# When batch 2's k is loaded, and when k's second piece is turned, in sliding-window attention with a gated feed-forward on one core

## The chip, the cores and the metric

The kernel runs on one core of one Trainium2 chip. The metric is the time of one execution on the device, in microseconds (us), and the figure that counts is the median of the runs. The core has engines that work side by side, each through its own queue in order: TensorE (PE, matrix products, with its weight loads PEld), VectorE (DVE), ScalarE (ACT), GpSimd (POOL) and SyncE (SP). In this kernel SP computes nothing. It issues transfers, and a transfer that waits on SP holds up every transfer behind it.

## The reference

Inputs q, k and v are [8 batches, 8 heads, 576 positions, 64] in float32.

```python
scores = scale * np.matmul(q, k.transpose(0, 1, 3, 2))      # scale = 1/8
mask = (rel >= 0) & (rel < 64)                               # rel = query position - key position
scores = np.where(mask, scores, -1000000000.0)
attn = exp(scores - max) / sum                               # softmax over the keys
o = np.matmul(attn, v)
x = o.transpose(0, 2, 1, 3).reshape(4608, 512)
h = x @ w_in                                                 # w_in 512 x 2048
out = (h * np.cos(h)) @ w_out                                # w_out 2048 x 512
```

A query sees only itself and the 63 positions before it. In blocks of 64 positions, a query block needs its own key block and the one before.

## The kernel before

**Two halves, interleaved.** The feed-forward runs over nine stages (`mt` 0 to 8) of 512 rows of x. A stage first makes h (line 443, `h_ps`) with the cosine gate (lines 589 and 592), and then the output product (line 604, `out_ps`). The attention of batch b is worked out inside an earlier stage: batch 1 inside the output product of stage 0, batch 2 inside that of stage 1, and so on. Its pieces are slipped between the matmuls by a list of planned times. `at(time, fn, ...)` puts a step on the list, and `pump(time)` calls whatever is due. A planned time is a place in the order only. It decides after which instruction a step stands on its engine, and nothing is held until that time on the chip.

**Groups.** The unit of attention is a pair of heads p and a query block j. Units are handled in groups of three or four. One group goes through these steps:

- scores on PE (line 305, `s_ps`), reading qT and kT, or qX and kX from batch 2 on
- masking and the row minimum on DVE (line 329, `s` and `negm`)
- the exponential with its sum on ACT (line 340, `e` and `den`)
- the reciprocal on DVE (line 347, `rden`)
- the normalisation `g_norm` on POOL (line 354, w = e * rden). The first three groups of batch 1 and the tail of batch 0 have it on DVE
- the transposition of w. Groups in the list `DIRECT` go through PE (line 363, `tw_ps`) and a copy on DVE. The others go through a transposing transfer from SP (line 366, `wT<-w`)
- the values product on PE (line 381, `o_ps`), copied as xT for the feed-forward stage

Groups are counted from `n_first`, so "group 9" of the change is the tenth counted from the tail of batch 0. It is a group of three units of batch 1, and it is the seventh group that POOL normalises after it has issued batch 2's q.

**Loading q and k.** From batch 2 on, `load_chunk` (line 159; issue at line 165) loads q and k of a batch in five chunks of 128 positions each. It is issued from POOL's queue. An issue takes POOL about 0.9 us, and the norms of line 354 stand in the same queue. `load_v` (line 168, issue at line 171) loads v the same way, after batch 1's norms. Part of v is then shifted by half a block (`v<-v`): for batch 1 by two transfers from SP (line 180), which the values product of stage 1 waits for.

**Turning.** `turn` (line 246, issue at line 250) transposes what was loaded, from SP: all of q as `qX` in one transfer of 20 blocks, then k as `kX` in two. The first piece holds chunks 0 and 1 (8 blocks), the second chunks 2 to 4 (12 blocks). The scores of a batch come in two lots. The first lot reads the first piece of kX alone, and the second lot, some 6 us later, reads the second piece as well. Before the change the first piece of k is planned just behind q, and the second for `t0 + 2.5`, a few steps later. In between stand the transposing transfers of the previous batch's last groups (two for batch 2, four in the later stages), and behind them the stores of the finished output (line 463).

**Where batch 2's k stood.** Batch 2's q chunks were planned from 4.0 in steps of 0.5, k's chunks 0 to 3 right behind them, and chunk 4 at 26.9. On POOL this gives: five q loads, four k loads, six norms of batch 1, the fifth k load, one norm (group 9), two norms, then v.

Of the kernel before, what the change touches and what calls it, by code (L numbers as in the profile page):

```python
# [40 lines left out]
T = 2 * Q  # L41
# [23 lines left out]
def kernel(  # L65
# [401 lines left out]
    def at(time, fn, *args):  # L467
        plan.append((time, len(plan), fn, args))
# [10 lines left out]
    for t in range(B - 1):  # L479
        last = max(i for i, units in enumerate(groups) if units[0][0] == t + 1)  # L480
        time = T * t + Q - 1.4
        for i in range(last + 1 - n):
            time += PACE * len(groups[n - 1]) if i else 0
            if t and i == 4:
                time = max(time, T * t + Q + 4.3)
# [16 lines left out]
    for b in range(1, B):  # L502
        t0 = T * (b - 1)
        if b > 1:
            for i, name in enumerate(("q", "k")):
                for c in range(NC):
                    time = 4 + 0.5 * (c + NC * i) if b == 2 else t0 - T + 8 + 0.9 * (c + NC * i)
                    if i and c > (3 if b == 2 else 1):
                        time = 26.9 if b == 2 else t0 - T + 22.5 + 1.5 * (c - 2)
                    at(time, load_chunk, name, b, c)  # L510
                for c, (lo, hi) in enumerate(((0, 2), (2, NC)) if i else ((0, NC),)):
                    at(t0 + 2.5 if c else t0 - (5.8 if b > 2 else 3.4) + 0.1 * i, turn, name, b, lo, hi)
            for c in range(5):
                at(t0 + 3.5 + 0.9 * c, load_v, b, c)
            for time, part in ((13.5, 0), (19.9, 2), (21.7, 3)):
                at(t0 + time, spread_v, b, part, None)
# [5 lines left out]
    for mt in range(1, n_mt):  # L522
        for p in range(PAIRS):
            time = max(ready[b, p - p % 2 + i // TU, j] for i in range(2 * TU) for b, j in (divmod(mt * TU + i % TU, NU),))
            time = max(time, 25.5) if mt == 1 else T * mt - (8.01 if mt == n_mt - 1 else 1.01)
# [118 lines left out]
```

## Time and profile before

| what | before |
|---|---|
| median of three runs | 306.38 us (304.9, 306.38, 306.77) |
| the profiled execution's own time | 305.0 us |
| its span, first to last instruction | 302.9 us |
| PE busy | 286.5 us, 95% of the span |
| ACT busy | 235.0 us, 78% |
| DVE busy | 221.4 us, 73% |
| POOL busy | 172.2 us, 57% |
| granted TensorE clock | 1.000 |
| software queue (loads from POOL) | 18.06 MB, 79.3% of 16 engines' span |
| hardware queue (transfers from SP) | 24.98 MB, 47.3% |

The profile is of one execution. Its own time stands 1.4 us under the median of the three runs, so a difference that is worked out inside the trace is applied to both. The span leaves out 2.1 us around the program. A timeline row has the start in us, the duration in us, the engine, the line, the operation and what is written and read, how many instructions are merged in the row, and in brackets the engine's idle time before it and what ended that. "x3" with one duration is the stretch that three instructions took together. An engine with a "q" (SPq) is the queue that issues: its duration is the issue, and the transfer lands later. The row "DMA to landing" gives the least, the median and the longest time from issue to landing of the transfers asked for.

### The profile page before, as it was taken

To read this page: it belongs to the slowest core of one execution; us is meant where nothing else is said; L and a number is where in the kernel's file an instruction comes from. 1 tells how busy PE (TensorE), PEld (TensorE's weight loads), DVE (VectorE), ACT (ScalarE), POOL (GpSimd) and SP (SyncE) were. 2 spreads that over 40 slices of the span, in tenths; PEclk is the share of its full clock that TensorE was granted. 3 is DMA by queue.
4 is the path that set the end of the run, shared out by engine and by line. 5 is a ranking of instruction groups with operands and counts; after the bars stand their busy time and mean duration, and the time that the engine had idled before them with its cause. 6 is when DMAs were issued, how large, how long until landed. Compare 5 with 4: busy or idle time off the path is not lost.

```text
span 302.9 us, 8058 instructions
## 1 busy us (share of the span) xinstructions
PE 286.5 (95%) x2726; PEld 148.4 (49%) x2762; DVE 221.4 (73%) x852; ACT 235.0 (78%) x783; POOL 172.2 (57%) x204
## 2 busy tenths in 40 slices
PE   3789997999999999999999999989999999999996
PEld 2568743544454445444544454444544454454443
DVE  3899897778967897789678967896789778236701
ACT  5897898678997799879987998799869996116600
POOL 8997369792799368945995599549803620000000
PEclk9999999999999999999999999999999999999999
DMA  8999999999999999999999999999993470012011
GB/s 171 172 197 210 207 163 164 115 145 142 220 164 144 177 181 173 131 184 195 93 159 151 232 154 162 141 220 161 171 198 119 89 176 16 3 69 72 0 69 69
DMA packets 164841, 43.75 MB, mean 144 GB/s; under 512 B 153920, under 2 KB 160064, under 8 KB 164800
## 3 DMA queue, kind: packets, MB, share of 16 engines
q0 software_dynamic: 99360, 18.06, 79.3%
q1 hardware_dynamic: 65296, 24.98, 47.3%
q8 instruction: 21, 0.34, 0.5%
q14 instruction: 20, 0.16, 0.2%
q10 hardware_dynamic: 144, 0.20, 0.2%
HBM read 36.70 MB, written 9.44 MB: 152 GB/s over the span
## 4 chain that ended last, share of the span: by engine, by line
PE 67%; DMA 15%; POOL 6%; DVE 6%; issue 4%; ACT 0%; SPq 0%; POOLq 0%; DVEq 0%
PE h_ps L443 31%; PE out_ps L604 28%; DMA v<-in_v_dram 5%; DMA kX<-k 4%; POOL w L354 4%; DMA k<-in_k_dram 3%; DMA v<-v 3%; PE o_ps L381 2%; DVE s L329 2%; PE s_ps L305 2%; PE out_ps L455 1%; POOL v L171 1%; DMA q<-in_q_dram 1%; DVE negm L325 1%; PE tw_ps L363 1%
## 5 line engine op out<-in xcount | busy, mean ns | idle before, releaser
L604 PE MATMUL out_ps<-w_out,gT 128*128 128x512 bf16 x542 | 124.0, 379 | 1.7 <-issue 1.3
L443 PE MATMUL h_ps<-xT,w_in 128*128 128x512 bf16 x497 | 111.0, 379 | 1.1 <-issue 0.2
L354 POOL TENSOR_TENSOR w<-e,rden 128x512 bf16<-128x512 f32 (+1 forms) x75 | 73.0, 984 | 59.9 <-DVE rden L347 56.3
L592 DVE TENSOR_TENSOR gT<-h_ps,sin 128x512 bf16<-128x512 f32 x128 | 84.9, 688 | 30.2 <-ACT sin L589 30.2
L340 ACT ACTIVATE e<-s,negm 128x128 f32<-128x128 f32 x256 | 99.2, 403 | 1.9 <-DVE negm L329 1.8
L589 ACT ACTIVATE sin<-h_ps 128x512 f32<-128x512 f32 x128 | 73.7, 599 | 28.6 <-PE h_ps L443 28.1
L604 PEld LDWEIGHTS <-gT 128*128 128x128 bf16 x560 | 52.7, 98 | 60.5 <-issue 0.4
L443 PEld LDWEIGHTS <-w_in 128*128 128x128 bf16 x512 | 49.9, 98 | 59.1
L329 DVE CUSTOM_DVE_ANT_0 s<-s_ps,mask 128x128 f32<-128x128 f32 x256 | 57.9, 283 | 1.9 <-PE s_ps L305 1.7
L340 ACT ACTIVATION_READ_ACCUMULATOR e<-s,negm 128x1 f32 x256 | 51.9, 203 | 0.0
L171 POOL DMA_DIRECT2D v<-in_v_dram x40 | 34.1, 870 | 6.6 <-DMA w_out<-in_moe_w_out_dram 4.2
L117 ACT COPY out_sb<-out_ps 128x512 f32<-128x512 f32 (+1 forms) x18 | 10.5, 582 | 24.9 <-PE out_ps L604 19.3
L165 POOL DMA_DIRECT2D k<-in_k_dram x30 | 26.4, 893 | 1.7 <-DMA v<-in_v_dram 1.6
L165 POOL DMA_DIRECT2D q<-in_q_dram x30 | 25.4, 886 | 3.1 <-DMA w_out<-in_moe_w_out_dram 3.1
L117 DVE CAST xT<-o_ps 128x512 bf16<-128x512 f32 x28 | 18.3, 679 | 9.6 <-PE o_ps L381 9.3
L117 DVE COPY out_sb<-out_ps 128x512 f32<-128x512 f32 x18 | 12.3, 681 | 14.9 <-PE out_ps L604 14.9
L329 DVE DVE_READ_ACCUMULATOR2_ANT negm<- 128x1 f32 x256 | 20.9, 82 | 0.0
L347 DVE RECIPROCAL rden<-den 128x4 f32<-128x4 f32 (+1 forms) x80 | 13.5, 171 | 9.6 <-ACT e L340 7.7
L420 PE MATMUL h_ps<-xT,w_in 128*128 128x256 bf16 x128 | 15.5, 273 | 0.0
L420 PEld LDWEIGHTS <-w_in 128*128 128x128 bf16 x128 | 12.0, 98 | 1.4
L117 DVE COPY v<-v 64x1024 bf16<-64x1024 bf16 (+1 forms) x19 | 11.4, 601 | 0.4
L426 ACT ACTIVATE sin<-h_ps 128x512 f32<-128x512 f32 x16 | 9.1, 597 | 2.9 <-PE h_ps L420 2.9
(60 smaller groups left out, 187.5 us busy)
## 6 DMA issues: line engine op xcount, KB each, us to landing
out_dram<-out_sb SPq DMA_DIRECT2D x16, 512.0 KB, 7.7
v<-in_v_dram POOLq DMA_DIRECT2D x32, 128.0 KB, 6.2
q<-in_q_dram POOLq DMA_DIRECT2D x24, 128.0 KB, 8.7
k<-in_k_dram POOLq DMA_DIRECT2D x24, 128.0 KB, 7.9
w_in<-in_moe_w_in_dram POOLq DMA_DIRECT2D x2, 768.0 KB, 11.1
w_out<-in_moe_w_out_dram POOLq DMA_DIRECT2D x1, 1024.0 KB, 12.9
w_out<-in_moe_w_out_dram POOLq DMA_DIRECT2D x2, 512.0 KB, 15.5
wT<-w SPq DMA_TRANSPOSE x58, 5.0
```

Source lines behind the costliest of these rows:

```text
L117: {"a": nc.scalar.copy, "p": nc.gpsimd.tensor_copy}.get(engine, nc.vector.tensor_copy)(out, in_)
L165: nc.gpsimd.dma_start(out=st[name, b][:n, c].rearrange("p (h d) -> p h d", h=H), in_=src.rearrange("h p d -> p h d"))
L171: nc.gpsimd.dma_start(out=vt.rearrange("p (h d) -> p h d", h=H), in_=v[b, :, c * 128:c * 128 + n, :].rearrange("h p d -> p h d"))
L329: nc.vector.tensor_tensor_reduce(out=s[:, u], in0=s_ps[:, u], in1=mask[:, 2 - j % 2 if j else 0], scale=-scale if b else -1.0, scalar=BIG, ...
L340: nc.scalar.activation(e[:, u], s[:, u], AF.Exp, bias=negm[:, u:u + 1], scale=1.0 if n < n_first else -1.0, accum_out=den[:, u:u + 1])
L347: nc.vector.reciprocal(out=rden[:, 0:len(groups[n])], in_=den[:, 0:len(groups[n])])
L354: (nc.gpsimd if engine == "p" else nc.vector).tensor_tensor(out=w[:, 0:u], in0=e[:, 0:u], op=ALU.mult, in1=rden[:, 0:u].unsqueeze(2).to_br ...
L420: nc.tensor.matmul(out=st["h0", i][:, e], lhsT=w_in_sb[:, ks, ff * 128:ff * 128 + 128], rhs=st["xT", 0][:, ks, half], start=ks + e == 0, s ...
L443: nc.tensor.matmul(out=st["h", ff], lhsT=w_in_sb[:, ks, ff * 128:ff * 128 + 128], rhs=st["xT", mt][:, ks], start=start, stop=stop)
L589: nc.scalar.activation(sin, h_ps, AF.Sin, bias=math.pi / 2.0)
L592: nc.vector.tensor_tensor(out=gt[:, e], in0=h_ps, in1=sin, op=ALU.mult)
L604: nc.tensor.matmul(out=o_ps[e], lhsT=gT[ff // 2][:, ff % 2, ms * 128:ms * 128 + 128], rhs=w_out_sb[:, ff], start=ff == 0, stop=ff == n_ff - 1)
```

## The change

Two conditions in the plan are altered. Batch 2's k chunks 0 to 3 no longer follow its q. All five are planned at 27.1 to 27.5. On POOL this puts all of them behind the seventh norm, that of group 9, and ahead of the last two norms of batch 1. And `turn` of k's second piece is planned 0.1 behind the first piece, in every stage, where it was planned for `t0 + 2.5`.

```diff
                     time = 4 + 0.5 * (c + NC * i) if b == 2 else t0 - T + 8 + 0.9 * (c + NC * i)
-                    if i and c > (3 if b == 2 else 1):
-                        time = 26.9 if b == 2 else t0 - T + 22.5 + 1.5 * (c - 2)
+                    if i and (b == 2 or c > 1):
+                        time = 27.1 + 0.1 * c if b == 2 else t0 - T + 22.5 + 1.5 * (c - 2)
                     at(time, load_chunk, name, b, c)
                 for c, (lo, hi) in enumerate(((0, 2), (2, NC)) if i else ((0, NC),)):
-                    at(t0 + 2.5 if c else t0 - (5.8 if b > 2 else 3.4) + 0.1 * i, turn, name, b, lo, hi)
+                    at(t0 - (5.8 if b > 2 else 3.4) + 0.1 * i + 0.1 * c, turn, name, b, lo, hi)
```

The order of the instructions on PE, DVE and ACT stays the same, instruction for instruction, and no instruction is added or taken away. The orders of POOL and SP become these:

```
POOL, batch 2     before: q x5, k x4, norm x6, k, norm, norm x2, v x5
                  after:  q x5, norm x7, k x5, norm x2, v x5
SP, batch 2       before: qX, kX first, wT x2, kX second, stores
                  after:  qX, kX first, kX second, wT x2, stores
SP, batches 3, 4, 6   before: qX, kX first, wT x4, kX second, stores
                      after:  qX, kX first, kX second, wT x4, stores
SP, batches 5, 7  before: qX, kX first, wT x4, kX second, stores
                  after:  qX, kX first, wT, kX second, wT x3, stores
```

## The prediction

> **What bounds the kernel now.** PE is busy 95% of the span, so I read PE's waits first: only what PE waits for can be won. The rows give the waiting work, the releaser, the total in us, the times and the longest.
>
> ```profile
> PE tw_ps L363 <- POOL w L354: 1.5, 3, 0.9
> ...
> PE s_ps L305 <- DMA kX<-k: 0.6, 1, 0.6
> ...
> PE o_ps L381 <- DMA v<-v: 0.4, 1, 0.4
> ```
>
> These three are the waits that the change can touch, 2.5 us together. Next, PE's timeline, for their places and for the times at which PE asks for what the change moves.
>
> ```profile
> 49.34 0.34 PE L363 MATMUL tw_ps<-ident,w 128*128 128x128 bf16 x3 [0.86 <-POOL w L354]
> 50.12 0.34 PE L363 MATMUL tw_ps<-ident,w 128*128 128x128 bf16 x3 [0.45 <-POOL w L354]
> ...
> 53.36 0.60 PE L381 MATMUL o_ps<-wT,v 128*64 128x64 bf16 x26 [0.44 <-DMA v<-v]
> ...
> 58.43 0.69 PE L381 MATMUL o_ps<-wT,v 128*64 128x64 bf16 x32
> ...
> 72.33 0.64 PE L305 MATMUL s_ps<-kX,qX 64*64 64x128 bf16 x32
> ...
> 78.19 0.75 PE L305 MATMUL s_ps<-kX,qX 64*64 64x128 bf16 x40
> ...
> 88.35 1.20 PE L381 MATMUL o_ps<-wT,v 128*64 128x64 bf16 x64
> ...
> 202.16 0.75 PE L305 MATMUL s_ps<-kX,qX 64*64 64x128 bf16 x40 [0.62 <-DMA kX<-k]
> ...
> 211.59 1.20 PE L381 MATMUL o_ps<-wT,v 128*64 128x64 bf16 x64
> ```
>
> PE stands 0.86 + 0.45 = 1.31 us for two norms of batch 1, 0.44 for the shifted v, and much later 0.62 for the second piece of kX. Now POOL, which does the norms and issues the loads.
>
> ```profile
> 44.86 3.54 POOL L165 DMA_DIRECT2D k<-in_k_dram  x4
> 48.46 2.39 POOL L354 TENSOR_TENSOR w<-e,rden 128x384 bf16<-128x384 f32 x3
> 51.09 0.83 POOL L354 TENSOR_TENSOR w<-e,rden 128x384 bf16<-128x384 f32 x1 [0.23 <-DVE rden L347]
> 52.18 1.61 POOL L354 TENSOR_TENSOR w<-e,rden 128x384 bf16<-128x384 f32 x2 [0.27 <-DVE rden L347]
> 53.73 0.74 POOL L165 DMA_DIRECT2D k<-in_k_dram  x1
> 54.67 0.83 POOL L354 TENSOR_TENSOR w<-e,rden 128x384 bf16<-128x384 f32 x1 [0.20 <-DVE rden L347]
> 57.04 2.04 POOL L354 TENSOR_TENSOR w<-e,rden 128x512 bf16<-128x512 f32 x2 [1.54 <-PE tw_ps L363]
> 59.02 4.26 POOL L171 DMA_DIRECT2D v<-in_v_dram  x5
> ```
>
> Three norms start with no wait right behind four k issues: they were ready and stood behind the issues.
>
> **Part 1, the norms ahead of k.** The reciprocal that the third norm needs is done at 47.97 + 0.17 = 48.14, those of the first two before it:
>
> ```profile
> 47.97 0.17 DVE L347 RECIPROCAL rden<-den 128x3 f32<-128x3 f32 x1
> ```
>
> With POOL free at 44.86 and 0.8 us a norm (2.39 / 3), the first two are done by 48.14, and the third by about 48.9. PE asks for the first at 49.34 - 0.86 = 48.48, and for the second at 49.67 less those 0.86. Both waits go: **-1.31 us**, if PE can use them. The next lock is the shifted v. In the chain of waits its transfer runs from 45.39 for 7.84 us, beside the four k loads; the landing row of these four follows.
>
> ```profile
> 45.39 7.84 DMA v<-v
> ...
> DMA to landing us min/median/max: 7.6/7.9/8.6
> ```
>
> It lands at 53.23, and PE would now ask at 53.36 - 0.44 - 1.31 = 51.61. If the landing stays, the whole 1.31 turns into a longer wait there, and the part is worth 0. If it comes by 51.61, the part is worth 1.31 + 0.44 = 1.75. Without the four k loads the engines have less to move from 44.86 on. If the k loads took half of the last 3.2 us (my estimate: two streams at the end of it), v lands near 51.6. That is the value I take.
>
> The next thing late is a `wT` that the last 32 value products at 58.43 need. Its norm is the sixth. Norms five and six need a reciprocal whose exponential is among the last of ACT's unbroken run:
>
> ```profile
> 50.42 0.40 ACT L340 ACTIVATE e<-s,negm 128x128 f32<-128x128 f32 x1
> ```
>
> That run ends near 50.9 and cannot start earlier, so the two norms end at about 51.2 + 1.61 = 52.8. SP issues the `wT` then, where it did so at 53.82:
>
> ```profile
> 53.82 2.55 SPq L366 DMA_TRANSPOSE wT<-w  x1
> 56.69 3.11 SPq L250 DMA_TRANSPOSE qX<-q  x1
> 59.95 1.26 SPq L250 DMA_TRANSPOSE kX<-k  x1
> 61.31 2.90 SPq L366 DMA_TRANSPOSE wT<-w  x2
> 64.39 5.77 SPq L250 DMA_TRANSPOSE kX<-k  x1
> ...
> 183.13 1.25 SPq L250 DMA_TRANSPOSE kX<-k  x1
> 184.48 5.92 SPq L366 DMA_TRANSPOSE wT<-w  x4
> 190.57 5.12 SPq L250 DMA_TRANSPOSE kX<-k  x1
> ```
>
> The landing row of the one at 53.82, and below it that of all `wT`:
>
> ```profile
> DMA to landing us min/median/max: 4.1/4.1/4.1
> ...
> DMA to landing us min/median/max: 2.3/5.0/9.2
> ```
>
> With 4.1 it lands at 56.9 to 57.0. PE, 1.75 earlier, asks at 56.68: 0.3 given back. Part 1 is worth **1.45 us** (0 to 1.75).
>
> **Part 2, k comes later.** The seventh norm needs a reciprocal behind the xT copy on DVE, which moves with PE. I put the norm at 52.9 to 53.7. The five k issues then run from 53.7 to about 58.0 (4 x 0.89 + 0.74). They cost PE nothing as long as kX is in time. The last two norms end at 60.0, and v is issued from 60.0, 1.0 later than before. v's cover: its landing row, and the DVE copy that reads chunks 1 to 3.
>
> ```profile
> DMA to landing us min/median/max: 6.2/7.1/9.0
> ...
> 72.81 0.67 DVE L117 COPY v<-v 64x1536 bf16<-64x1536 bf16 x1
> ```
>
> Chunk 3 issued at 62.7 lands at 69.8, or 71.7 with the longest; the copy stands at 72.81 - 1.45 = 71.4. So v costs 0, or 0.3 us at the worst of its own rows.
>
> For kX the rows of k: the lone fifth load of before, at 53.73, and all chunk loads; then the second piece at 64.39, and all turns.
>
> ```profile
> DMA to landing us min/median/max: 4.0/4.0/4.0
> ...
> DMA to landing us min/median/max: 3.4/8.3/15.4
> ...
> DMA to landing us min/median/max: 11.8/11.8/11.8
> ...
> DMA to landing us min/median/max: 3.8/6.9/11.8
> ```
>
> The first piece needs chunk 1, issued at 54.6: in at 58.6 (4.0) to 62.9 (8.3). With 6.9 its turn lands at 65.5 to 69.8, and PE asks at 72.33 - 1.45 = 70.88: in time. The second piece needs chunk 4, issued at 57.2: in at 61.2 to 65.5. SP, free of the two `wT` that stood ahead, issues it at about 62 to 66. Even with the 11.8 of before, it lands at 74 to 77.8, against 78.19 - 1.45 = 76.74. I take 4.0 to 6 for the k loads, since POOL issues no other load between 48 and 59, and a landing at 75: cost **0** (0 to 1.1 by the median load, 7.7 by the longest).
>
> [...]
>
> **Part 3, the second turn ahead of the `wT`.** At 183.13 the first piece is issued, and the second, 7.4 us later, lands so that PE stands 0.62 us. Issued at about 184.4 with the longest landing of 11.8 it is in by 196.2, four us ahead of 200.1 (202.16 - 0.62 - 1.45): **-0.62 us**. What it displaces: four `wT`, each later by the 5.12 of that issue at most. The last, issued before 190.4, then goes at 195.5 and lands with 9.2 at 204.7, and its values product stands at 211.59. For batch 2, two `wT` are issued by 72 and land by 81 against 88.35. The stores behind them stay where they were, since the same issues stand ahead of them. SP may wait for k's last chunk in front of the `wT`; the margins of 7 us cover that.
>
> **The sum.** -1.45 - 0.62 = -2.07 us. On the profiled execution that is 305.0 - 2.1 = 302.9 us. The median of the runs is 1.4 above that execution, so 306.38 - 2.1 = **304.3 us**, 0.7% less. The most that these edits can win is 1.31 + 0.44 + 0.62 = 2.37 us.
>
> **The rivals.**
> - *k too late (slower).* The place is the second lot of batch 2's scores. Any landing of the second piece after 76.74 is a stall; from 76.74 + 2.07 = 78.8 on the kernel is slower than before. With the longest k landing, chunk 4 is in at 57.2 + 15.4 = 72.6, the turn lands at 84.4, PE stalls 7.7 us, and the time is 306.38 - 2.1 + 7.7 = 312.0. For it: v and q loads follow k in the same queue, and the turn took 11.8 here. Against it: 15.4 is the largest of all chunk loads, and the lone load of this place took 4.0.
> - *The same, small.* A landing between 76.74 and 78.8 eats part of the gain: 304.3 to 306.4, about 305.4.
> - *The shifted v does not hurry.* If v lands at 53.23 anyway, part 1 is worth 0, and only the 0.62 stays: 305.8. For it: 7.84 us may be the transfer's own time beside q loads.
>
> **How the numbers follow.** Forecast 0.52, small lateness 0.18, v unhurried 0.18, k too late 0.12. The three runs spread by 1.9 us, and 1% (3.1 us) is about what a measurement of this kernel can tell from no change. The forecast's gain lies inside that, and only the runs' spread or a gain outside these edits carries it below 303.3: faster 0.17. Of k too late, and of losses that I have not seen, 0.13 goes over 309.4. The rest, 0.70, is within. The range takes in 2.37 with some spread (302.6), and above the forecast the small lateness, v unhurried and the near half of the slower rival (308.0).
>
> **What would show it.** Right: no wait of `tw_ps` on POOL near 48 to 50, `v<-v` in by about 51.7, the five k issues at 53.7 to 58, the second kX in before 76.7, no wait at the scores near 200, all later stages shifted by 1.4 to 1.8. Wrong: PE waiting for kX at either lot of batch 2's scores, or for v at 51.6, or for a `wT` at the last values, or a new wait on a displaced store or `wT`.

## The result and the profile after

The changed kernel takes 302.35 us (median of five executions) where the kernel before takes 306.38. The ratio is 0.9893, with a 95% interval of 0.9857 to 0.9929. The ratios here and below leave out executions more than 1.5% longer than the fastest of the same kernel (here the one of 307.52 us), which the medians keep. The profiled executions compare like this: 305.0 us before and 302.35 after, spans 302.9 and 300.6. Between these two traces the gain is therefore 2.3 us, against 2.07 forecast. The medians are 4.0 apart, and where the rest comes from is told below.

PE's waits in the changed kernel (waiting work, releaser, total us, times, longest):

```profile
PE o_ps L381 <- DMA v<-v: 0.3, 1, 0.3
...
PE tw_ps L363 <- POOL w L354: 0.2, 1, 0.2
```

Of the 2.5 us of three waits, 0.5 is left, and kX is in the list no more. PE's timeline at the places of the prediction:

```profile
48.49 0.50 PE L363 MATMUL tw_ps<-ident,w 128*128 128x128 bf16 x6
...
51.74 0.60 PE L381 MATMUL o_ps<-wT,v 128*64 128x64 bf16 x26 [0.29 <-DMA v<-v]
...
56.81 0.69 PE L381 MATMUL o_ps<-wT,v 128*64 128x64 bf16 x32
...
70.71 0.64 PE L305 MATMUL s_ps<-kX,qX 64*64 64x128 bf16 x32
...
76.57 0.75 PE L305 MATMUL s_ps<-kX,qX 64*64 64x128 bf16 x40
...
86.74 1.20 PE L381 MATMUL o_ps<-wT,v 128*64 128x64 bf16 x64
...
199.85 0.75 PE L305 MATMUL s_ps<-kX,qX 64*64 64x128 bf16 x40
```

The two transpositions that stood 0.86 and 0.45 us now run as one piece. The later rows stand 1.6 us earlier than before (58.43 to 56.81, 72.33 to 70.71), and near 200, where PE no longer waits, they come to stand 2.3 us earlier (202.16 to 199.85). POOL and SP in the same stretch:

```profile
46.84 2.54 POOL L354 TENSOR_TENSOR w<-e,rden 128x384 bf16<-128x384 f32 x3 [1.55 <-DVE negm L329]
49.71 0.83 POOL L354 TENSOR_TENSOR w<-e,rden 128x384 bf16<-128x384 f32 x1 [0.33 <-DVE rden L347]
51.77 2.40 POOL L354 TENSOR_TENSOR w<-e,rden 128x384 bf16<-128x384 f32 x3 [1.23 <-DVE negm L329]
54.11 4.26 POOL L165 DMA_DIRECT2D k<-in_k_dram  x5
```

```profile
45.07 1.29 SPq L180 DMA_DIRECT2D v<-v  x2
50.56 4.03 SPq L366 DMA_TRANSPOSE wT<-w  x2
54.90 4.16 SPq L250 DMA_TRANSPOSE qX<-q  x1
63.00 4.99 SPq L250 DMA_TRANSPOSE kX<-k  x2
68.09 3.36 SPq L366 DMA_TRANSPOSE wT<-w  x2
```

The norms now wait for their inputs, with POOL free ahead of them. On SP the gap between the end of qX's issue (59.06) and 63.00 is the wait for k's chunk 1. The landing rows, in this order: the shifted v, the five k loads, and the second turn of kX for batch 2:

```profile
DMA to landing us min/median/max: 5.9/5.9/5.9
...
DMA to landing us min/median/max: 3.9/7.8/8.3
...
DMA to landing us min/median/max: 8.6/8.6/8.6
```

The shifted v takes 5.9 us where it took 7.84. Issued second at about 45.75, it lands at 51.6. The second kX is issued at 65.4 and lands at 74.0, 2.6 us ahead of PE.

### The profile page after: what moved, and what is told of

It reads as the page before. It is cut to its first block, busy times and chain, and to the rows that moved or that the text cites. A ratio compares the mean times of both kernels' runs of the same rounds, so it can differ in the third digit from the quotient of the medians.

```text
span 300.6 us, 8056 instructions
## 1 busy us (share of the span) xinstructions
PE 286.6 (95%) x2726; PEld 148.8 (50%) x2762; DVE 221.4 (74%) x852; ACT 234.5 (78%) x783; POOL 172.1 (57%) x204
## 4 chain that ended last, share of the span: by engine, by line
PE 78%; DMA 10%; DVE 4%; POOL 3%; issue 3%; SPq 0%; ACT 0%; POOLq 0%; DVEq 0%
PE h_ps L443 36%; PE out_ps L604 34%; DMA v<-in_v_dram 5%; DMA k<-in_k_dram 3%; PE s_ps L305 3%; PE o_ps L381 2%; DMA v<-v 2%; POOL w L354 2%; PE out_ps L455 1%; DVE xT L117 1%; DVE s L329 1%; PE tw_ps L363 1%; PE tk_ps L214 0%; DVE qT L236 0%; DVE negm L325 0%
## 5 line engine op out<-in xcount | busy, mean ns | idle before, releaser
L340 ACT ACTIVATION_READ_ACCUMULATOR e<-s,negm 128x1 f32 x256 | 48.1, 188 | 0.0
L117 ACT COPY out_sb<-out_ps 128x512 f32<-128x512 f32 (+1 forms) x18 | 10.2, 565 | 24.9 <-PE out_ps L604 19.3
```

The costliest lines, as they stand in the source:

```text
L117: {"a": nc.scalar.copy, "p": nc.gpsimd.tensor_copy}.get(engine, nc.vector.tensor_copy)(out, in_)
L340: nc.scalar.activation(e[:, u], s[:, u], AF.Exp, bias=negm[:, u:u + 1], scale=1.0 if n < n_first else -1.0, accum_out=den[:, u:u + 1])
```

## The experiments

The theory was the prediction's: PE waited for norms that stood behind k's issues, then for a shifted v that shared the DMA engines with k, and later for a turn that stood behind four `wT`. The rivals were that one of the two edits alone carries the gain, that the shifted v takes its own time, and that late loads are made up.

In the table, "full clock" is the median of those executions whose mean granted TensorE clock was above 0.997, and "lower" counts those with 0.984 to 0.994. The ratios are against the kernel before, timed on the same chip in the same rounds.

| run | median us | ratio, interval | full clock | lower |
|---|---|---|---|---|
| before, in three rounds of runs | 305.83, 305.40, 304.98 | | 304.89, 304.88, 304.59 | 18 of 29, 9 of 29, 10 of 28 |
| changed kernel, repeated | 303.13 | 0.9911 (0.9884 to 0.9938) | 303.13 | 0 of 6 |
| k loads only | 304.51 | 0.9982 (0.9954 to 1.0010) | 304.03 | 4 of 12 |
| turn only | 304.61 | 0.9972 (0.9949 to 0.9995) | 304.43 | 5 of 12 |
| norms on DVE | 304.75 | 0.9979 (0.9952 to 1.0005) | 304.44 | 4 of 12 |
| k behind all norms | 305.90 | 0.9984 (0.9956 to 1.0012) | 304.54 | 8 of 12 |
| k behind v | 313.39 | 1.0252 (1.0221 to 1.0282) | none | 5 of 5 |
| q behind the fourth norm | 306.34 | 1.0015 (0.9982 to 1.0047) | 305.19 | 6 of 12 |
| filler on PE | 305.59 | 1.0008 (0.9984 to 1.0033) | 305.59 | 0 of 12 |
| q behind the third norm | 307.73 | 1.0065 (1.0031 to 1.0099) | 304.54 | 10 of 12 |
| changed kernel, repeated | 302.57 | 0.9913 (0.9885 to 0.9941) | 302.57 | 0 of 11 |
| k split | 303.15 | 0.9927 (0.9900 to 0.9954) | 303.15 | 0 of 12 |

**The changed kernel again.**

> The changed kernel once more, beside its parts. Both theories: ratio to before near 0.989, time 302.1 to 303.3 us, no wait of tw_ps on POOL near 48 to 50, v<-v in near 51.6, no wait for kX.

The time held. But the profiled execution, the longest of the six at 303.96 us, shows PE waiting 1.60 us for the shifted v, where the first one showed 0.29:

```profile
53.31 0.60 PE L381 MATMUL o_ps<-wT,v 128*64 128x64 bf16 x26 [1.60 <-DMA v<-v]
```

There v itself had come later, so that the shift was issued at 47.03 and 47.71, not 45.07 and 45.75, and it landed at 53.17 although it took only 5.5 us. PE's row stands at 53.31, where the kernel before had it at 53.36: in this execution v eats all that the norms had won. So the shifted v is the lock that is left. The three profiles of the changed kernel fit the view that its landing spreads the executions (302.35 us with a wait of 0.29, 303.96 with 1.60, 304.18 with 1.64), but three traces do not show it for the others.

**One part alone: the loads.**

```diff
-                    if i and c > (3 if b == 2 else 1):
-                        time = 26.9 if b == 2 else t0 - T + 22.5 + 1.5 * (c - 2)
+                    if i and (b == 2 or c > 1):
+                        time = 27.1 + 0.1 * c if b == 2 else t0 - T + 22.5 + 1.5 * (c - 2)
```

> Only batch 2's k loads are moved; the second turn stays where it was. Main theory (norms, then the shifted v, are worth about 1.7 us; the turn order is worth the rest): the first h of stage 1 starts 1.6 to 1.8 us earlier than before, but the second piece of kX is now issued behind two wT at about 67 and lands at 76 to 79, against 76.57: PE waits 0 to 2.4 us for it at batch 2's second lot, and 0.6 or more again near 200. Time 304.0 to 306.0. Rival (the whole gain comes with the loads, the turn order is worth nothing): as the changed kernel, 302.1 to 303.3, no wait for kX.

Its waits:

```profile
PE o_ps L381 <- DMA v<-v: 1.1, 1, 1.1
PE s_ps L305 <- DMA kX<-k: 0.9, 1, 0.9
```

As the theory had it, k loaded late and turned behind two `wT` is too late for batch 2's second lot: 0.86 us at 77.98. The wait near 200, which should have come back with the old place of the second turn, did not:

```profile
201.21 0.75 PE L305 MATMUL s_ps<-kX,qX 64*64 64x128 bf16 x40
```

The second piece landed at 200.77 here and at 202.03 in the kernel before, and PE had lost 0.86 us on the way. Without that loss it would have asked at 200.35 and waited 0.4 us.

**One part alone: the turn.**

```diff
-                    at(t0 + 2.5 if c else t0 - (5.8 if b > 2 else 3.4) + 0.1 * i, turn, name, b, lo, hi)
+                    at(t0 - (5.8 if b > 2 else 3.4) + 0.1 * i + 0.1 * c, turn, name, b, lo, hi)
```

> Only the second turn is moved; batch 2's k loads stay. Main theory: the waits of 0.86 and 0.45 for POOL's norms and 0.44 for v<-v stay, the 0.62 for kX near 202 goes: 0.6 us less than before, 305.8. Rival (the turn order relieves the queue in every stage and carries most of the gain): 303.5 or less.

At full clock the gain is 0.46 us (304.43 against 304.89), near the 0.6 of the theory and far from the rival's. The medians are 1.2 apart, as fewer executions had the lower clock (5 of 12 against 18 of 29). The wait for the norms stays, larger in this execution, and PE comes so late that it does not wait for v:

```profile
PE tw_ps L363 <- POOL w L354: 2.8, 3, 2.2
```

kX is gone from PE's waits, but that alone does not show what the early turn is worth near 200. The loads-only kernel and two below (norms on DVE, filler on PE) keep the old turn, and their profiles show no wait there either: the piece landed at 200.77, 201.88 and 202.56, and PE asked at 201.21, 202.01 and 202.73. The old order is 0.1 to 0.4 us on the safe side or, as in the kernel before, 0.5 late. The early turn lands more than 7 us ahead in every profile that has it.

The parts are worth 0.86 and 0.46 us at full clock, together 1.3. The whole is worth 1.8 to 2.0 in the same comparisons (304.89 to 303.13, 304.59 to 302.57). With 6 to 11 executions of each changed kernel that spread by 1 to 3 us, the difference is not clear of chance. What the traces do show is one direction: the late k needs the early turn, or PE waits 0.86 us at batch 2's second lot.

**Is the shifted v a lock, and do the k loads slow it?** The k loads stay, and the first two of the norms that POOL did go to DVE.

```diff
-                at(time + lag, fn, n, *("d" for _ in range(1) if fn is g_norm and n < n_first + 3))
+                at(time + lag, fn, n, *("d" for _ in range(1) if fn is g_norm and n < n_first + 5))
```

> The k loads and the turns stay as before; the two norms that PE waited for are done on DVE instead of POOL, so that PE no longer waits for them while the four k loads still run beside the shifted v. Main theory (the shifted v is slowed by the k loads and is the next lock): the waits of 0.86 and 0.45 go, v<-v still lands near 53.2, PE waits there 1.3 to 1.8 us in place of 0.44, and the time stays within 0.3 us of before. Rival (the queue behind POOL is all, v is no lock): 1.3 us less, 305.1.

```profile
PE o_ps L381 <- DMA v<-v: 1.3, 1, 1.3
PE o_ps L381 <- DMA wT<-w: 0.3, 1, 0.3
PE tw_ps L363 <- POOL w L354: 0.2, 1, 0.2
...
DMA to landing us min/median/max: 5.9/6.5/7.1
```

The norms no longer hold PE, and the wait moves to v, which lands at 53.23, as before, after 7.1 us. The gain at full clock is 0.45 us, more than the 0.3 expected and a third of the rival's 1.3. Taking the norms out of POOL's queue is not enough. The k loads have to leave v's side.

**How late may k be?** Twice later than in the change, with the turn of batch 2's k planned behind the loads (that line of the edit is left out here).

```diff
-                        time = 27.1 + 0.1 * c if b == 2 else t0 - T + 22.5 + 1.5 * (c - 2)
+                        time = 31.5 + 0.1 * c if b == 2 else t0 - T + 22.5 + 1.5 * (c - 2)
```

> Batch 2's k is loaded behind all nine norms instead of seven, and its turns behind the two wT. Main theory (k has a margin of 1.4 us at the first lot of scores and 2.6 at the second, and costs PE nothing inside it): the issues run from about 57.4 to 61.6, the first piece lands at about 72.6, PE waits 1 to 3 us for kX at batch 2's first lot, and the time is 1 to 3 us over the changed kernel, 303.5 to 305.5. Rival (loads wait for nothing that PE needs; anything before 70 is in time): as the changed kernel.

> Batch 2's k is loaded behind v as well, and turned behind the stores. Main theory: the issues run from about 61.7 to 65.9, the first piece lands near 77, PE waits 5 to 9 us for kX at the first lot of batch 2, nearly all of it is lost, and the time is 307.5 to 312, slower than before. Rival (a late load is made up later): under 305.

The second of the two has 39.2 in place of 31.5. The timeline of PE in the first and, below it, in the second:

```profile
74.42 0.64 PE L305 MATMUL s_ps<-kX,qX 64*64 64x128 bf16 x32 [3.45 <-DMA kX<-k]
```

```profile
80.50 1.07 PE L305 MATMUL s_ps<-kX,qX 64*64 64x128 bf16 x32 [9.85 <-DMA kX<-k]
```

In the profiled executions, issues that start 3.5 us later (57.59 instead of 54.11) cost a stall of 3.45 us, and issues that start 7.8 us later (61.93) one of 9.85. The margin of the change is small, and PE's later rows keep the delay. Both stalls were larger than expected by about 0.5 to 0.9 us: the first turn took 9.0 and 8.2 us there and not 6.3, and in the second kernel the loads took 9.2 to 9.6. The first kernel's median of 305.90 is above its range of 303.5 to 305.5. Its four executions at full clock took 302.88 to 304.63, so by these times their stall was smaller than that of the profiled one (307.73). The second kernel's 313.39 is above its range too: the stall is followed by a spell at half the clock, seen in the windows (stretch, its length, PE busy with the number of instructions, the same for PEld, DVE, ACT and POOL, granted clock, DMA share, GB/s).

```profile
70.60:80.50 9.90, 0.05 (x2) 0.03 (x2) 1.84 (x3) 2.08 (x3) 4.54 (x6) 0.68 2.52 146
80.50:84.00 3.50, 3.50 (x38) 1.71 (x39) 2.71 (x25) 2.44 (x13) 0.00 (x0) 0.50 1.08 113
84.00:92.00 8.00, 7.79 (x72) 3.78 (x73) 5.33 (x40) 6.69 (x33) 4.32 (x4) 0.98 0.18 35
```

As an estimate, 302.35 + 9.85 is 312.2, and 3.5 us at half speed cost 1.75, less the 0.29 that v no longer costs: 313.7, where the profiled execution took 313.93. The profiled execution of the first kernel has such a spell as well, from 75.72 on (mean clock 0.994): fifteen output products from 74.99 on take 5.10 us there, where 23 take 5.13 in the changed kernel.

**The lower clock.** The same spell is in the profiled execution of the turn-only kernel, behind its longer wait for the norms (2.22 us):

```profile
49.26:52.67 3.41, 0.89 (x7) 0.55 (x9) 0.66 (x4) 2.27 (x12) 3.35 (x5) 1.00 1.74 180
52.67:56.08 3.41, 3.31 (x22) 1.36 (x24) 1.38 (x11) 1.26 (x6) 2.24 (x4) 0.50 1.79 123
```

PE was busy 0.89 of 3.41 us, and then got half the clock (0.50) for 3.41 us. Of the thirteen profiled executions, five have a mean clock under 0.997: turn only, k behind all norms, q behind the fourth norm and q behind the third norm with 0.994, and k behind v with 0.984. The other eight have 0.999 or 1.000. In the first four, the 3.41 us before the spell hold 0.89 us of PE's work (turn only), 1.30 (k behind all norms), 1.33 (q behind the fourth norm) and 1.53 (q behind the third norm). So PE did not stand idle throughout before these spells. In k behind v the clock falls during the wait of 9.85 us (0.68 over that stretch), and by its windows above half the clock lasts about 10.2 us. Two stretches with nearly the same work are q behind the third norm, with the half clock right behind, and, below it, the second repetition of the changed kernel with its wait of 1.64 us, where the full clock stays:

```profile
87.68:91.09 3.41, 1.53 (x63) 1.15 (x63) 1.37 (x3) 3.06 (x7) 3.07 (x5) 1.00 2.96 123
91.09:94.50 3.41, 3.41 (x20) 1.36 (x16) 0.69 (x1) 0.00 (x0) 3.41 (x5) 0.50 1.31 185
```

```profile
49.85:53.26 3.41, 1.77 (x52) 1.05 (x50) 1.55 (x13) 3.41 (x20) 1.98 (x3) 1.00 0.41 84
53.26:56.67 3.41, 3.41 (x27) 1.72 (x21) 3.28 (x15) 1.83 (x10) 2.59 (x4) 1.00 0.20 36
```

There, 1.53 us of work was followed by half the clock and 1.77 was not. In the profiled execution of the kernel before, at full clock, no stretch of that length, wherever it is begun from 10 us on, has less than 1.86 us up to PE's last product (10.93 to 14.34), and the 3.41 us from 48.00, with the two waits for the norms, hold 2.05. That the executions of that kernel with the lower clock waited longer than the profiled one, as the turn-only execution did, is my estimate; none of them was traced, and the expectation below has its "right after these waits" from the turn-only trace. Nor was one of the loads-only kernel or of the norms-on-DVE kernel, which had the lower clock 4 times in 12 without a wait for the norms in their profiles, so where their spells stand is not shown.

To test whether PE's idle time is the cause, the kernel before was given work in its wait: eight transpositions of the identity, which nobody reads, ahead of the two late w.

```diff
-            for i in range(u):
-                nc.tensor.transpose(t_ps[:, i], w[:, i], ident)
+            for i in range(-8 if n in (n_first + 3, n_first + 4) else 0, u):
+                nc.tensor.transpose(t_ps[:, max(i, 0)], ident if i < 0 else w[:, i], ident)
```

> The kernel before, with eight transpositions of the identity that nobody reads ahead of each of the two w that PE waited for, so that PE works while it waits. Theory of the clock (some executions of the kernel before were granted half the clock for one spell of 3.4 us right after these waits, which the changed kernel does not show): hardly any of its executions, 2 of 12 at most, has a mean clock of 0.993 to 0.994, where 18 of 29 of the kernel before had it; at full clock the time is 304.9 plus 0 to 0.6. Rival (the lower clock has nothing to do with PE's idle time there): about half of the executions show it again.

None of 12 executions had the lower clock. The kernel before had it in 9 of 29 in the same rounds, and in 37 of 86 in all three; chance alone would give 0 of 12 beside 9 of 29 about 3 times in 100. At full clock the filler costs 0.7 us (305.59), slightly over the expected 0.6, so it is not a gain on the whole. The profiled execution even waits longer than the one of before, at full clock throughout:

```profile
48.22 0.61 PE L363 MATMUL tw_ps<-ident 128*128 128x128 bf16 x8
50.46 0.34 PE L363 MATMUL tw_ps<-ident,w 128*128 128x128 bf16 x3 [1.63 <-POOL w L354]
50.64 0.61 PE L363 MATMUL tw_ps<-ident 128*128 128x128 bf16 x8
```

The 3.41 us from 48.45, around that wait, hold 1.73 us of PE work, about 1.0 of it filler.

**The changed kernel once more.**

> The changed kernel once more, for the count of executions with a lower mean clock. Theory of the clock (PE's long waits of stage 0 are gone, so the spell at half the clock goes): at most 1 of 6 again, and 301.7 to 304 us. Rival (the low share so far was chance): about half.

None of 11, where the kernel before had 10 of 28 in the same rounds; with the first executions and the first repetition that is 1 of 22. The profiled execution, the longest of the eleven at 304.18 us, waits 1.64 us for v and 0.66 for a `wT` of batch 2.

**Can v hurry more?** The changed kernel with batch 2's last two q chunks later.

```diff
-                    time = 4 + 0.5 * (c + NC * i) if b == 2 else t0 - T + 8 + 0.9 * (c + NC * i)
+                    time = (4 + 0.5 * (c + NC * i) if c < 3 else 25.5) if b == 2 else t0 - T + 8 + 0.9 * (c + NC * i)
```

> The changed kernel with batch 2's last two q chunks behind the fourth norm, so that fewer loads run beside the shifted v. Main theory (v<-v shares the DMA engines with the loads, and is what PE waits for now): v<-v takes 4.5 to 5.3 us instead of 5.5 to 5.9, PE's wait for it shrinks by 0.3 to 1 us, and the time is 0.3 to 1 us less than the changed kernel; norms four to seven are 0.4 to 1.7 us later without cost. Rival (v<-v's time is its own): v<-v still takes 5.5 us or more, no gain, or a loss where a later norm makes a wT late.

The landing of the shifted v, and then PE's waits:

```profile
DMA to landing us min/median/max: 3.8/3.9/3.9
```

```profile
PE o_ps L381 <- DMA wT<-w: 2.1, 2, 1.9
```

The mechanism was right and the forecast wrong. v takes 3.9 us, less than expected, and PE does not wait for it at all. But what PE wins there it gives back at 91.5 to batch 2's own `wT`, with interest. To learn whether the later k was to blame, the same two chunks went behind the third norm (24.5 in place of 25.5), which leaves k's issues at 54.07 to 58.32:

> As the run with the last two q chunks behind the fourth norm, but behind the third, where POOL has more idle time, so that k's five issues stay at about 54 to 58. That run had v<-v in at 3.9 us and lost 1.92 us later to four wT whose transfers were late. If the loss came from k and v being issued 1 us later: v<-v near 4.0 to 4.5 us, no wait of the values product near 88, 301.5 to 303 us. If PE simply arrives earlier than the transfers allow (the DMA engines are the next limit): again a wait for wT of 1 us or more near 88 to 92, and 304 to 306 us.

```profile
57.91 0.41 PE L381 MATMUL o_ps<-wT,v 128*64 128x64 bf16 x14 [1.14 <-DMA wT<-w]
...
90.94 0.46 PE L381 MATMUL o_ps<-wT,v 128*64 128x64 bf16 x12 [1.88 <-DMA wT<-w]
...
PE o_ps L381 <- DMA wT<-w: 3.0, 2, 1.9
```

The same wait near 91 again, and 10 of 12 executions at the lower clock. So the later k was not needed for it. The median of 307.73 is above the expected 304 to 306; the two executions at full clock (304.34, 304.74) lie inside. The other 1.14 us went to the `wT` that the last values of batch 1 need, in at 57.86. The rows of the last of the four `wT` that batch 2's values product needs, in the kernel before and, below, in the changed kernel and in this one:

```profile
L366 SPq DMA_TRANSPOSE wT<-w x1: 1851/1851/1851, 82.4 to 82.4; - x1
...
DMA to landing us min/median/max: 4.7/4.7/4.7
```

```profile
L366 SPq DMA_TRANSPOSE wT<-w x1: 1816/1816/1816, 80.8 to 80.8; - x1
...
DMA to landing us min/median/max: 5.8/5.8/5.8
```

```profile
L366 SPq DMA_TRANSPOSE wT<-w x1: 2737/2737/2737, 82.0 to 82.0; - x1
...
DMA to landing us min/median/max: 8.9/8.9/8.9
```

The landings are 87.1, 86.6 and 90.9. The 53rd of the 64 products is the first to need this transfer, and PE asks for it at 89.20, 87.58 and 89.06. The margin goes from 2.1 us to 1.0 to a wait of 1.9. In the first repetition of the changed kernel it was 0.15, and in the second a wait of 0.66. That PE simply arrives earlier does not explain it: here it asks 1.5 us later than in the first profile of the changed kernel, and the transfer takes 8.9 us in place of 5.8. Batch 3's loads, issued from about 65 on, are slower too, 9.5 to 15.8 us in place of 6.7 to 14.0. qX's landing took 10.8 us, little more than the 9.9 to 10.7 of the changed kernel. Which transfer slows the `wT` is not shown.

**A version with more room.**

```diff
-                        time = 27.1 + 0.1 * c if b == 2 else t0 - T + 22.5 + 1.5 * (c - 2)
+                        time = (25.5 if c < 2 else 27.1) + 0.1 * c if b == 2 else t0 - T + 22.5 + 1.5 * (c - 2)
```

> The changed kernel with k's chunks 0 and 1 behind the fourth norm and chunks 2 to 4 behind the seventh, to use the time near 51 to 55 in which little is transferred. Main theory: the first piece of kX is in by 67 and all later loads come about 1.3 us earlier, which widens margins that PE does not wait at: the same time as the changed kernel within 0.5 us, 302 to 303.5. If k's first chunks still run beside v<-v, up to 0.5 us more. Rival (the changed kernel still loses to late transfers somewhere): 1 us less or better.

kX's first piece landed at 66.9 where it had been 69.3 to 71.2 in the changed kernel's profiles, and the time is that of the changed kernel within the scatter (303.15 beside 302.57, 0.58 more where 0.5 was allowed, and inside the 302 to 303.5). PE did not wait there, so room there is worth nothing. No version tried beats the change.

## Why the prediction was right, point by point

- *The norms, -1.31.* Right. Both waits are gone, and the two transpositions run together at 48.49. All three profiles of the changed kernel show it, and in each PE gains 1.6 us there, counted by its own rows.
- *The shifted v by 51.6.* The step that all of part 1 hung on. It came out in the first profile (in at 51.61), with a wait of 0.29 that the prediction had at 0, since PE asked at 51.45. The norms-on-DVE run shows that v had to come earlier: with k beside it, the wait only moves. The reason given for the rival "v does not hurry", that 7.84 us is the transfer's own time, falls, for without k it takes 5.5 to 6.2 us in the three profiles of the changed kernel. But the rival's outcome is real: in the two other profiles of the changed kernel v landed at 53.17 and 52.63, because its shift was issued 2.0 and 0.7 us later, PE waited 1.60 and 1.64, and most of part 1 was lost. That the first profile met 51.6 to the hundredth is luck, and the estimate behind it (half of the last 3.2 us) rested on no row.
- *The `wT` that gives back 0.3.* Mis-sized. It was issued at 53.41, 0.6 later than forecast, but landed after 2.29 us and not the 4.1 of the row of before (in at 55.69), so nothing was given back. That is 0.3 more than forecast. The norms gave 0.3 more as well, v 0.3 less, and the changed execution was 0.17 late before it came to the change: together they turn 2.07 into the 2.3 of the first pair of traces. The other two traces, both of executions at the long end, gain 0.7. The medians at full clock, 1.8 to 2.0 apart, are the better measure of the forecast, and they bear it out.
- *k's loads and kX in time.* Right in the result, with two errors that offset each other: the loads took 3.9 to 8.3 us and not 4 to 6, and the second turn 8.6 and not 11.8. It landed at 74.0, forecast 75. The 4.0 came from the row of a lone load, and of a half one: the fifth chunk holds the last 64 of the 576 positions (64 KB), not 128. Of the five in a row only the first was as quick, at 3.9 us with 128 KB; the four behind it took 7.7 to 8.3. The two runs with later k priced the slower rival: it was real, and it began about 1.4 us further on, the margin of the first lot (69.3 against 70.7). The prediction had looked for it at the second lot, which has 2.6 us; there it came only in the loads-only run, with the late turn. Inside these margins the later issues of the changed kernel (54.11 and not 44.86) cost PE nothing; beyond the first, issues at 57.59 cost the stall of 3.45 us.
- *The second turn, -0.62.* Right in the first profile. It is issued at 182.9, lands at 191.1, and there is no wait at 199.85. But three later profiles with the old turn show no wait there either, so 0.62 is what this wait costs in some executions; alone, the turn was worth 0.46. In batch 2 the prediction counted on the early turn ("free of the two `wT`") without a price for it: the loads-only run gives 0.86.
- *What is displaced.* The two `wT` moved behind the turn were in by 77.5, with room. But the last of the next four, whose place did not change, had 1.0 us left where it had 2.1 before, and was late in the second repetition. The prediction had no term for them.
- *The clock.* Missed. The prediction carried the 1.4 us between the profiled execution, which ran at full clock, and the median over to the changed kernel unchanged, and gave no reason. 37 of 86 executions of the kernel before had a lower mean clock, and their median is 1.3 to 1.9 us longer (304.9 to 306.2, 304.6 to 306.45), about what a spell at half the clock costs (1.7 us, estimated from the 3.41 us at 0.50 in the turn-only trace); of the changed kernel it was 1 of 22. This fits the 4.0 us between the medians, and the median of 302.35, which stands 0.25 below the low end of the range, while the ratio applied to 306.38 gives 303.1. The chance of 0.17 for less than 303.3 left it out too; the repetitions, with ratios of 0.9911 and 0.9913, come to 303.7.

## What to carry to other kernels

When a wait goes, look for the next lock and ask whether the same edit moves it too: here moving four loads freed an engine's queue and, more than that, the transfer that ran beside them. Late loads and their consumer's place in its queue belong to one decision: the loads alone left PE a new wait of 0.86 us. And when PE is nearly full, count what its clock does after its idle spots, in several executions, and not in the profiled one alone: here a wait of 2.22 us was followed by 3.41 us at half the clock (turn only), and one of 1.64 by the full clock (the second repetition). The same holds for a gain: the three profiles of the changed kernel gave 2.3, 0.7 and 0.7 us.

## What the runs showed of the hardware

In four traces PE was granted half the clock behind 3.41 us in which it had been busy 0.89 (turn only), 1.30 (k behind all norms), 1.33 (q behind the fourth norm) and 1.53 us (q behind the third norm). The spell took 3.41 us in turn only. In the second repetition of the changed kernel, 1.77 us of work in 3.41 was followed by the full clock (1.00). Sixteen small transpositions in the wait, 1.2 us of work, went with 0 low executions of 12, where the kernel before had 9 of 29 in the same rounds. A shifting transfer between two places of the on-chip memory (the second of the two) took 3.9 us behind three loads (q behind the fourth norm), 5.5 to 6.2 behind five (the three profiles of the changed kernel), and 7.1 and 7.84 where four more loads were issued beside it (norms on DVE and the kernel before).
